# Twenty block products instead of twenty-two: the first layer of the last two experts as a rank-20 scheme

## The chip, the core and the metric

The kernel runs on one core of one Trainium2 chip. The metric is device time in microseconds of one execution. A core has TensorE (PE, with its weight loads PEld), VectorE (DVE), ScalarE (ACT), GpSimd (POOL) and SyncE (SP, here only a DMA queue). SBUF is the working memory, PSUM the eight banks into which matmuls accumulate.

## The reference, cut to what matters

A recurrent attention gives x (3072 tokens, 384 features); a mixture of four experts follows. The change touches only the second part, for experts 2 and 3:

```python
def _moe_ref(x, domain_probs, w1, w2) -> np.ndarray:
    N, D = x.shape                       # 3072, 384
    E = w1.shape[0]                      # 4 experts, 1024 hidden features each
    p = domain_probs / (domain_probs.sum(-1, keepdims=True) + 1e-09)
    out = np.zeros((N, D), dtype=np.float32)
    for e in range(E):
        h = np.maximum(x @ w1[e], 0.0)
        out += p[:, e:e + 1] * (h @ w2[e])
    return out.astype(np.float32)
```

All is float32. Each factor is split into a high part in a rounded format (F32R) and a low part, the rest; a product of two factors is three matmuls: high x high, low x high, high x low.

## The kernel before

**Two phases.** The first computes the attention and, beside it, experts 0 and 1 in blocks of 256 tokens (w1_step for the first layer, w2_step for the second; each step's second layer is issued one step late, and `mo.flush` issues the last). Sums of experts are kept in DRAM (acc_d). The second phase, from about 596 us on, does experts 2 and 3.

**Second phase.** Tokens come in blocks of 384 (TB2). A row R is a pair of such blocks for one expert; there are 4 rows per expert (NB2), 8 in all (NR2), R = 0 to 3 for expert 2 and R = 4 to 7 for expert 3. The 1024 hidden features are 8 tiles of 128. `unit(R, j)` takes two of these tiles and the pair of token blocks: a 2 x 3 matrix of 128 x 128 weight blocks times a 3 x 2 matrix of 128 x 384 blocks of x. Done directly that is 12 block products; a scheme with prepared sums of blocks (s1 to s4 of weights, t1 to t4 of x) needs 11. Each is `prod`, three matmuls of 384 columns. ScalarE and VectorE move partial results between four PSUM banks (a, b, c, d) and apply the ReLU: `hi_h` writes the high part of a hidden tile (ScalarE), `lo_h` the low part (VectorE).

**Second layer.** `l2(R, u, f)` multiplies one hidden tile of one token block by its second-layer weights: 9 matmuls into three output banks; after the eighth tile of a block VectorE adds the result, times the expert's probability, to the accumulator, which goes to acc2_d (expert 2, a GpSimd DMA) or out (expert 3, SP).

**Order.** All matmuls of the phase, and after the prologue all ScalarE and VectorE operations and the SP loads, are pinned in the order of the code. `fill(k)` puts an `l2` of an earlier unit between the products of a unit: four per unit from R = 1 on, two in row 0 and none in its first unit. The rest of the work, the preparation of weights (`prep_w`: loads, sums, splits) and of the next row's x (`prep_x`), stands in a list, `side`; `bg(n)` takes n steps from it at fixed points of a unit (`room`, `xat`, `late`). A split is a ScalarE copy to the high part and a VectorE subtraction for the low part. All weights of expert 2 and the x of row 0 are prepared in the prologue, beside the last block of the first phase. X's parts have two buffers each, hidden tiles twelve, PSUM has four banks for products and four for outputs.

Of the kernel before, what the change touches and what calls it, by code (L numbers as in the profile page):

```python
# [8 lines left out]
F32 = mybir.dt.float32  # L9
# [55 lines left out]
DMA_SCRATCH = 4096  # L65


def fast_path(ctx, tc, qkP, aP, vP, probsP, w, out, flag):
# [760 lines left out]
    with ExitStack() as c2:  # L829
        fin = c2.enter_context(tc.tile_pool(name="fin", bufs=2))  # L830
        ps_h2 = c2.enter_context(tc.tile_pool(name="ps_h2", bufs=2, space=PSUM))
        ps_o2 = c2.enter_context(tc.tile_pool(name="ps_o2", bufs=2, space=PSUM))
        acc2_d = [dram.tile([P, HD], F32, name=f"acc2_d{c}") for c in range(NT // P)]
        NP = FE // 2
        NR2 = (E - E1) * NB2
        pairs, shared = {}, {}
        count = {"h": 0, "o": 0, "w": 0}
        held = {"on": False}

        def cut(n):  # L840
            return slice(n * P, (n + 1) * P)

# [6 lines left out]
        def act(dst, src, fn=AF.Copy):  # L849
            pin(nc.scalar.activation(dst, src, fn))  # L850
# [7 lines left out]
        def split(hi, lo, src):  # L858
            return "split", (lambda: act(hi, src)), (lambda: tt(lo, src, hi, ALU.subtract))

        side = []

        def bg(n):
            while n > 0 and side:
                kind, first, second = side.pop(0)
                if kind == "split":
                    first()
                if kind != "sum" and side and side[0][0] == "split":
                    side[0][1]()
                    side[0] = ("rest",) + side[0][1:]  # L870
                second()
                n -= 1

        def stage2(i):
            tag = MID[count["w"] % len(MID)]
            count["w"] += 1
            return moe.tile([P, 2 * HD], F32, tag=tag, name=f"w2st{count['w']}", bufs=1 if tag == "x" else None)

        def prep_w(e, j):
            i = e * FE + 2 * j  # L880
            sts = []
            for u in range(2):
                st = stage2(i + u)
                pin(nc.sync.dma_start(st, w[i + u]))
                sts.append(st)
            st0, st1 = sts
            s = stage2(i)[:, :4 * P]
            if j % 2 == 0:
                shared[e] = [wpool.tile([P, 2 * HD], F32R, tag=f"w{nm}", name=f"s{nm}{i}") for nm in ("hi", "lo")]
            (h0, l0), (h1, l1) = ([wpool.tile([P, 2 * HD], F32R, tag=f"w{nm}", name=f"w{nm}{i + u}")  # L890
                                   for nm in ("hi", "lo")] for u in range(2))
            hs, ls = (x[:, (j % 2) * HD:(j % 2 + 1) * HD] for x in shared[e])

            def both(hi, lo, n):
                return hi[:, cut(n)], lo[:, cut(n)]

            pairs[e, j] = dict(a11=both(h0, l0, 0), a12=both(h0, l0, 1), a13=both(h0, l0, 2),
                               s4=both(h1, l1, 0), a22=both(h1, l1, 1), a23=both(h1, l1, 2),
                               s1=both(hs, ls, 0), s2=both(hs, ls, 1), s3=both(hs, ls, 2))
            wts[i], wts[i + 1] = (h0, l0), (h1, l1)  # L900

            def sums():
                tt(s[:, cut(0)], st1[:, cut(0)], st1[:, cut(1)], ALU.add)
                tt(s[:, cut(1)], s[:, cut(0)], st0[:, cut(0)], ALU.subtract)
                tt(s[:, cut(2)], st0[:, cut(0)], st1[:, cut(0)], ALU.subtract)
                tt(s[:, cut(3)], st0[:, cut(1)], s[:, cut(1)], ALU.subtract)

            return [("sum", None, sums), split(h0, l0, st0), split(h1[:, P:], l1[:, P:], st1[:, P:]),
                    split(hs, ls, s[:, :3 * P]), split(h1[:, cut(0)], l1[:, cut(0)], s[:, cut(3)])]

        def load_x2(R):
            xs = []
            for u in range(2):
                b = 2 * (R % NB2) + u
                x = fin.tile([P, NJ, TB2], F32, tag="x2", name=f"xb{R}_{u}", bufs=2)
                c = b * C2
                while c < (b + 1) * C2:
                    n = min(CG - c % CG, (b + 1) * C2 - c)
                    o = (c - b * C2) * P
                    pin(nc.sync.dma_start(x[:, :, o:o + n * P],  # L920
                                          y_d[c // CG].rearrange("(j p) t -> p j t", p=P)
                                          [:, :, c % CG * P:(c % CG + n) * P]))
                    c += n
                xs.append(x)
            return xs

        def prep_x(R, xs, X):
            (b11, b21, b31), (b12, b22, b32) = ([x[:, k, :] for k in range(NJ)] for x in xs)

            def put(nm, src):  # L930
                X[nm] = (fin.tile([P, TB2], F32R, tag="xoh", name=f"xh{R}_{nm}", bufs=9),
                         fin.tile([P, TB2], F32R, tag="xol", name=f"xl{R}_{nm}", bufs=9))
                return split(*X[nm], src)

            t2, t3 = (fin.tile([P, TB2], F32, tag=nm, name=f"{nm}_{R}", bufs=1) for nm in ("t2", "t3"))
            yield [("sum", None, lambda: tt(t3, b22, b12, ALU.subtract)),
                   ("sum", None, lambda: tt(b12, b12, b11, ALU.subtract)),
                   ("sum", None, lambda: tt(t2, b22, b12, ALU.subtract))]
            yield [put("b11", b11), put("t1", b12)]
            yield [put("t2", t2), put("b21", b21)]  # L940
            yield [("sum", None, lambda: tt(b21, b21, t2, ALU.subtract)), put("t3", t3), put("b22", b22)]
            yield [put("b31", b31), put("b32", b32), put("t4", b21)]

        def prod(ps, W, X, start=False, stop=False):
            (wh, wl), (xh, xl) = W, X
            for n, (a, b) in enumerate(((wh, xh), (wl, xh), (wh, xl))):
                pe(ps, a, b, start=start and n == 0, stop=stop and n == 2, skip_group_check=True)

        def claim(ps):
            pe(ps, pairs[E1, 0]["a11"][0], X["b11"][0], start=True, stop=True, skip_group_check=True)  # L950

        def bank(R, j, nm):
            count["h"] += 1
            return (ps_h, ps_h2)[count["h"] % 2].tile([P, TB2], F32, tag="ph", name=f"phb{R}_{j}{nm}")

        def temp(R, j, nm):
            return fin.tile([P, TB2], F32, tag="tmp", name=f"{nm}_{R}_{j}", bufs=5)

        hid = {}

        def hi_h(R, u, f, src):
            hh = fin.tile([P, TB2], F32R, tag="hh2", name=f"hhb{R}_{u}_{f}", bufs=12)
            act(hh, src, AF.Relu)
            hid[R, u, f] = hh, src
# [7 lines left out]
        def unit(R, j, X, fill, at):  # L972
# [5 lines left out]
            if R == 0 and j == 0:  # L978
                claim(b)
# [306 lines left out]
```

## Time and profile before

| | us |
|---|---|
| median of 3 runs | 992.63 (992.56 to 994.05) |
| the profiled execution | 992.13 |
| its span, first to last instruction | 990.4 |
| start of the second phase's matmuls | about 596.4 |
| the last matmul's end | about 984.1 |

The profiled execution is one run; its span leaves out 1.7 us around the program. Mean granted TensorE clock is 0.998. In rows of instruction groups the numbers are: count, busy time in us, mean ns of one, idle time of the engine before them and who ended it. In rows of single instructions they are: start in us, duration, engine, line, operation, tiles; idle time before it and its releaser stand in square brackets.

### The profile page before, as it was taken

What the parts mean: (1) busy time and instruction counts of PE and PEld (TensorE: products, weight loads), DVE (VectorE), ACT (ScalarE), POOL (GpSimd) and SP (SyncE); (2) the same over time, 40 slices, a digit from 0 to 9 for tenths busy, and PEclk for the clock granted to TensorE, in tenths of its full rate; (3) what the DMA queues carried; (4) which work ended last, traced back from release to release, by engine and by line L of the source; (5) the groups of instructions that cost most, each with busy time, mean ns of one, the idle gap of its engine ahead of it and who ended that gap; (6) DMA issues with size and microseconds to landing.
All of it is one profiled execution on the core that took longest, in us unless ns stands there. A gap on an engine that the chain in (4) does not pass through costs nothing.

```text
span 990.4 us, 17208 instructions
## 1 busy us (share of the span) xinstructions
PE 962.9 (97%) x6812; PEld 938.9 (95%) x6812; DVE 667.6 (67%) x1458; ACT 440.0 (44%) x856; POOL 52.7 (5%) x90
## 2 busy tenths in 40 slices
PE   5899998999999999999999999999999999999997
PEld 2799998999999999999999999999999999999997
DVE  7889989898888989878862374646454654444431
ACT  7755535355363643627232364434343534333320
POOL 6030000000000000000000000000000000000000
PEclk9999999999999999999999999999999999999999
DMA  9585276584665738366381453224131323131111
GB/s 312 170 172 138 71 188 144 142 190 123 176 157 136 179 129 208 107 167 175 74 184 17 130 154 116 72 67 133 49 118 59 107 70 96 48 96 49 49 48 51
DMA packets 102440, 120.63 MB, mean 122 GB/s; under 512 B 6928, under 2 KB 87872, under 8 KB 102352
## 3 DMA queue, kind: packets, MB, share of 16 engines
q1 hardware_dynamic: 95472, 98.83, 36.2%
q0 software_dynamic: 6880, 20.63, 8.5%
q8 instruction: 55, 0.90, 0.4%
q14 instruction: 33, 0.27, 0.1%
HBM read 78.81 MB, written 40.62 MB: 121 GB/s over the span
## 4 chain that ended last, share of the span: by engine, by line


## 5 line engine op out<-in xcount | busy, mean ns | idle before, releaser
L198 PE MATMUL po<-whi,hh 128*128 128x384 f32 x384 | 129.6, 338 | 1.1 <-ACT hh L188 1.1
L198 PE MATMUL po<-wlo,hh 128*128 128x384 f32 x384 | 128.9, 336 | 0.0
L847 PE MATMUL pob<-whi,hlb 128*128 128x384 f32 x384 | 128.3, 334 | 0.0
L847 PE MATMUL pob<-whi,hhb 128*128 128x384 f32 x384 | 128.3, 334 | 0.0
L847 PE MATMUL pob<-wlo,hhb 128*128 128x384 f32 x384 | 128.3, 334 | 0.0
L198 PE MATMUL po<-whi,hl 128*128 128x384 f32 x384 | 124.3, 338 | 1.0 <-DVE hl L189 1.0
L188 ACT ACTIVATE hh<-ph 128x512 fp32r<-128x512 f32 x96 | 57.1, 594 | 145.4 <-PE ph L178 142.8
L178 PE MATMUL ph<-xha,whi 128*128 128x256 f32 x576 | 103.9, 286 | 1.2 <-ACT xha L165 1.2
L178 PE MATMUL ph<-xha,wlo 128*128 128x256 f32 x576 | 101.3, 283 | 0.0
L178 PE MATMUL ph<-xla,whi 128*128 128x256 f32 x576 | 100.9, 284 | 0.4 <-DVE xla L167 0.4
L189 DVE SCALAR_TENSOR_TENSOR hl<-ph,hh 128x512 fp32r<-128x512 f32 x96 | 66.0, 688 | 44.2 <-ACT hh L188 43.6
L178 PEld LDWEIGHTS ph<-xha,whi 128*128 128x128 f32 x576 | 85.9, 190 | 2.5 <-ACT xha L165 1.5
L178 PEld LDWEIGHTS ph<-xla,whi 128*128 128x128 f32 x576 | 82.5, 191 | 0.6 <-DVE xla L167 0.6
L178 PEld LDWEIGHTS ph<-xha,wlo 128*128 128x128 f32 x576 | 82.8, 190 | 0.2 <-issue 0.2
L198 PEld LDWEIGHTS po<-whi,hh 128*128 128x128 f32 x384 | 72.4, 189 | 1.5 <-ACT hh L188 1.3
L198 PEld LDWEIGHTS po<-whi,hl 128*128 128x128 f32 x384 | 70.9, 188 | 2.3 <-DVE hl L189 2.2
L198 PEld LDWEIGHTS po<-wlo,hh 128*128 128x128 f32 x384 | 72.5, 189 | 0.0
L847 PEld LDWEIGHTS pob<-whi,hhb 128*128 128x128 f32 x384 | 72.1, 188 | 0.0
L847 PEld LDWEIGHTS pob<-wlo,hhb 128*128 128x128 f32 x384 | 72.1, 188 | 0.0
L847 PEld LDWEIGHTS pob<-whi,hlb 128*128 128x128 f32 x384 | 72.1, 188 | 0.0
L532 PE MATMUL sc<-Qst,Kst 112*128 112x128 f32 x384 | 49.9, 280 | 0.8 <-DMA Qst<-q_d 0.3
L559 ACT ACTIVATE y<-yp 48x512 f32<-48x512 f32 (+1 forms) x42 | 24.9, 592 | 55.5 <-PE yp L553 55.2
(384 smaller groups left out, 1979.9 us busy)
## 6 DMA issues: line engine op xcount, KB each, us to landing
qk<-qkP SPq DMA_DIRECT2D x24, 384.0 KB, 6.9
acc_d<-acc POOLq DMA_DIRECT2D x24, 384.0 KB, 4.8
acc<-acc_d SPq DMA_DIRECT2D x48, 192.0 KB, 2.5
A<-aP SPq DMA_DIRECT2D x22, 384.0 KB, 8.1
w2st<-w SPq DMA_DIRECT2D x16, 384.0 KB, 3.8
xb<-y_d SPq DMA_DIRECT2D x16, 384.0 KB, 4.4
q_d<-Q SPq DMA_DIRECT2D x12, 387.0 KB, 4.1
Qst<-q_d SPq DMA_DIRECT2D x12, 387.0 KB, 5.9
```

What stands on the lines that cost most here:

```text
L178: ins = nc.tensor.matmul(ph[:, u, :], wt[:, j * P:(j + 1) * P], xt[:, j, :], start=(n == 0), stop=(n == 3 * NJ - 1))
L188: wts["hh"] = nc.scalar.activation(hh, ph, AF.Relu)
L189: nc.vector.scalar_tensor_tensor(hl, ph, 0.0, hh, op0=ALU.max, op1=ALU.subtract)
L198: nc.tensor.matmul(po[t], ht[:, u, t * P:(t + 1) * P], wt[:, HD:], start=(i % FE == 0 and n == 0), stop=(i % FE == FE - 1 and n == 2))
L532: ins = nc.tensor.matmul(s_ps[:, h, :], Kc[:, hf * 4 + h, :], Qc[:, hf * 4 + h, :], start=True, stop=True)
L559: state["y", g, c] = nc.scalar.activation(y[us, :, cs], y_ps[us], AF.Copy)
L847: return tc.keep_in_program_order(nc.tensor.matmul(*args, **kw))
```

## The change

Only the second phase changes.

- A unit now takes four feature tiles and the pair of token blocks: a 4 x 3 matrix of weight blocks times a 3 x 2 matrix of blocks of x, as 20 products (before: two units of 11). XOF says which of 16 prepared parts of x a product uses; UNIT is the order of one unit, written out: `M` product (number, bank, whether it starts the bank), `C` ScalarE copy, `D` VectorE sum, `H` and `L` the high and low parts of a hidden tile, `F` one `l2`, `B` steps from the side list. A unit has 20 `M`, 8 `C`, 10 `D`, 8 `H`, 8 `L`, 8 `F`.
- The first unit, (0, 0), has no `l2`; its first `F` is the flush.
- Of the sums of x, 12 per row, all are on GpSimd and not pinned; 16 splits per row. The parts X have one buffer each: a part is split anew (`need`, `freed`) only after its last product in the row's second unit.
- `prep_w` prepares the first-layer weights of one half expert: 4 loads, 14 block sums, 6 splits; its second-layer weights come by a GpSimd DMA, a negating ScalarE copy and an accumulating GpSimd DMA. Only the first half of expert 2 is prepared in the prologue; the second half in unit (0, 0), expert 3's halves in units (1, 0) and (4, 0).
- Raw weights, their sums, raw x and the sums of x share one tile, Z. In those three units the x of the next row is loaded behind the weights' steps in the side list; what is left in the list is drained at the end of each unit with h = 0.
- Five PSUM banks for products, three for outputs, each fixed; hidden tiles in a ring of eleven.

```diff
+XOF = (0, 1, 2, 3, 4, 5, 6, 7, 0, 8, 9, 6, 10, 11, 12, 13, 14, 15, 5, 9)
+UNIT = (
+    ("M", 19, 0, True), ("C", 1, 0),
+    ("M", 10, 2, True),
+    ("F",), ("B", 3),
+    ("M", 6, 0, False), ("C", "A", 0),
+    ("M", 11, 1, False), ("C", 3, 1), ("B", 2),
+    ("F",), ("D", 4, "A", "-", 2),
+    ("M", 1, 0, False), ("C", "B", 0),
+    ("M", 7, 3, False), ("H", 2, 0, 3),
+    ("M", 16, 1, False), ("C", "D", 1), ("L", 2, 0, 3),
+    ("F",), ("B", 3),
+    ("M", 12, 4, False), ("H", 0, 0, 4),
+    ("M", 3, 2, False), ("D", "B", "B", "-", 2),
+    ("M", 17, 0, False), ("C", "C", 0, -1.0), ("L", 0, 0, 4),
+    ("M", 8, 1, False), ("C", "E", 1),
+    ("F",), ("B", 4),
+    ("M", 13, 2, False), ("D", 3, 2, "-", "D"), ("D", "F", 2, "-", "E"),
+    ("M", 0, 0, True), ("C", "A", 0),
+    ("M", 2, 1, True), ("D", 4, 1, "+", "C"),
+    ("F",), ("D", 2, "A", "-", 1), ("B", 2),
+    ("M", 9, 3, False), ("H", 1, 0, 3),
+    ("M", 5, 0, False), ("L", 1, 0, 3), ("D", "F", "F", "-", 0),
+    ("F",), ("D", 1, 0, "+", "B"), ("H", 1, 1, "F"), ("B", 2),
+    ("M", 15, 4, False), ("H", 3, 0, 4),
+    ("M", 18, 2, False), ("L", 1, 1, "F"), ("L", 3, 0, 4), ("D", 3, 2, "+", "E"),
+    ("F",), ("D", "C", "C", "-", 2), ("B", 3),
+    ("M", 14, 1, False), ("H", 0, 1, 1), ("H", 3, 1, "C"),
+    ("F",), ("L", 0, 1, 1), ("L", 3, 1, "C"),
+    ("M", 4, 3, False), ("H", 2, 1, 3), ("B", 2), ("L", 2, 1, 3),
+)
...
+        Z = fin.tile([P, 11 * TB2], F32, name="Z")
+        X = [tuple(fin.tile([P, TB2], F32R, name=f"x{nm}{n}") for nm in ("h", "l")) for n in range(16)]
...
+        def pool(dst, x, y, op):
+            nc.gpsimd.tensor_tensor(dst, x, y, op=op)
...
         def bg(n):
-            while n > 0 and side:
-                kind, first, second = side.pop(0)
+            while side:
+                kind, need, first, second = side[0]
+                if need is not None and need not in freed:
+                    return
+                if kind != "pool" and n <= 0:
+                    return
+                if kind == "gap" and first > 0:
+                    side[0][2] -= 1
+                    return
+                side.pop(0)
+                if kind == "gap":
+                    continue
+                if kind in ("pool", "sum", "act"):
+                    first()
+                    n -= kind != "pool"
+                    continue
                 if kind == "split":
                     first()
-                if kind != "sum" and side and side[0][0] == "split":
-                    side[0][1]()
-                    side[0] = ("rest",) + side[0][1:]
+                if side and side[0][0] == "split" and (side[0][1] is None or side[0][1] in freed):
+                    side[0][2]()
+                    side[0][0] = "rest"
                 second()
                 n -= 1
...
+        def prep_w(e, h, base, raw, sums):
...
+            out = [step(*[(u,) for u in range(4)], on=load), ["gap", None, 2, None],
+                   step((n(0, 4), raw[:, :, 1], raw[:, :, 0], sub)),
+                   step((n(10, 12), raw[:, 2, :2], raw[:, 3, :2], add), (s[:, 8], a(1, 3), a(4, 3), add)),
+                   step((s[:, 9], a(2, 3), a(3, 3), add), (n(4, 6), n(0, 2), raw[:, :2, 2], add)),
+                   step((n(6, 8), n(0, 2), n(8, 10), add), (s[:, 5], s[:, 5], a(4, 3), sub)),
+                   step((s[:, 12], a(1, 2), a(2, 1), add), (s[:, 8], s[:, 12], s[:, 8], add),
+                        (s[:, 9], s[:, 12], s[:, 9], sub)),
+                   step((s[:, 10], s[:, 6], s[:, 10], sub), (s[:, 11], s[:, 7], s[:, 11], add)),
+                   step((s[:, 13], a(3, 1), a(4, 2), add), (s[:, 14], a(3, 1), a(1, 2), sub))]
+            for src, q, lim in ((n(0, 6), 0, slice(0, 6)), (n(6, 12), 1, slice(0, 6)), (n(12, 15), 2, slice(0, 3)),
+                                (raw[:, 2, 0::2], 2, slice(3, 5)), (a(2, 1), 2, 5)):
+                out.append(split(blocks(hi[q], lim), blocks(lo[q], lim), src))
+            out.append(split(blocks(ext, slice(0, 2)), blocks(ext, slice(2, 4)), raw[:, 3, 1:3], mark=("w", e, h)))
...
+                def minus(d_hi=d_hi, d_lo=d_lo, k=i + u):
+                    nc.gpsimd.dma_start(d_hi, w[k][:, HD:])
+                    act(d_lo, d_hi.bitcast(F32), scale=-1.0)
+                    nc.gpsimd.dma_start(d_lo, w[k][:, HD:], accum_op=ALU.add)
...
+        def prep_x(R):
+            b11, b21, b31, b12, b22, b32, v7, v6, v9, ta, tb = (Z[:, wide_cut(n)] for n in range(11))
...
+            return [step((R,), on=load_x2),
+                    g((v7, b11, b21, add), (ta, b12, b31, add), (v6, b22, b32, sub), (v9, b31, v6, add),
+                      (tb, b11, b31, add)),
+                    put(9, v7), put(6, b31), put(1, ta, True),
+                    g((ta, v7, v6, sub), (b31, b31, b32, sub), (b32, b12, b32, add)),
+                    put(7, b21), put(14, v9, True),
+                    g((b21, b21, v9, sub), (v7, v7, b12, sub)),
+                    put(10, tb, True),
+                    g((tb, v7, b22, sub)),
+                    put(3, ta), put(15, b12),
+                    g((b11, b12, b11, sub)),
+                    put(11, v6), put(0, b31), put(8, b21), put(12, b32), put(2, v7), put(5, tb), put(13, b11),
+                    put(4, b22)]
...
+        late_w = {(0, 0): (E1, 1, 5), (1, 0): (E1 + 1, 0, 10), (NB2, 0): (E1 + 1, 1, 0)}
+        freed.update(range(16))
+        side += prep_x(0)
+        drain()
+        side += prep_w(E1, 0, 0, SN[:, :4 * HD], ACC[:, :15 * P])
+        drain()
         held["on"] = True
...
+            for h in range(2):
+                if h == 1 or R > 0:
+                    acc_load(R if h == 1 else R - 1, 1 - h)
+                if (R, h) in late_w:
+                    e, q, base = late_w[R, h]
+                    side += prep_w(e, q, base, Z[:, :4 * HD], Z[:, 4 * HD:4 * HD + 15 * P])
+                if h == 0 and R + 1 < NR2:
+                    todo_x = prep_x(R + 1)
+                    side += todo_x[:2]
+                elif R + 1 < NR2:
+                    freed.clear()
+                    side += todo_x[2:]
+
+                def fill(k, first=(R == 0 and h == 0)):
+                    if not first:
+                        l2()
+                    elif k == 0:
+                        mo.flush()
+
+                unit(R, h, fill)
+                if h == 0:
+                    drain()
+        acc_load(NR2 - 1, 1)
+        for _ in range(FE):
+            l2()
```

## What I predict and why

> **What bounds the kernel now.** I read the busy shares first, then the stretches, then TensorE's waits, then single instructions. The page of the kernel before:
>
> ```profile
> span 990.4 us, 17208 instructions
> PE 962.9 (97%) x6812; PEld 938.9 (95%) x6812; DVE 667.6 (67%) x1458; ACT 440.0 (44%) x856; POOL 52.7 (5%) x90
> PE   5899998999999999999999999999999999999997
> DVE  7889989898888989878862374646454654444431
> ```
>
> TensorE is busy in nearly every slice; VectorE falls to about half of that in the second phase (from slice 24). The stretches split the second phase into its first row of blocks (R = 0) and a little of the next, and the rest; the last is the exit. Columns: stretch, length, then busy time and count of TensorE's matmuls, its weight loads, VectorE, ScalarE and GpSimd, the granted clock, DMA share and GB/s.
>
> ```profile
> 596.40:648.80 52.40, 51.59 (x290) 49.85 (x290) 27.11 (x54) 24.66 (x53) 2.50 (x4) 1.00 0.28 85
> 648.80:984.10 335.30, 335.30 (x1935) 334.99 (x1933) 159.76 (x312) 119.46 (x255) 11.23 (x21) 1.00 0.23 73
> 984.10:990.40 6.30, 0.01 (x1) 0.00 (x0) 0.67 (x2) 0.00 (x0) 0.00 (x0) 0.90 0.30 101
> ```
>
> From 648.8 on TensorE never pauses: 335.30 / 1933 weight loads = 0.1735 us per matmul, whatever it multiplies. So a matmul taken out is worth 0.1735 us as long as the other engines keep up. The waits of TensorE from 560 on are two, both tiny, and one of the phase's few gaps shows how a chain through VectorE stalls it in the first row, where little second-layer work is there to fill:
>
> ```profile
> PE phb_3b L847 <- DVE phb_3c L853: 0.3, 1, 0.3
> 605.38 0.19 PEld L847 LDWEIGHTS phb_1d<-xh_t,shi 128*128 128x128 f32 x1 [0.45 <-DVE mq L853]
> ```
>
> **The change, part by part. Matmuls.** Before, the phase issues 32 pairs x 33 = 1056 first-layer matmuls, 2 that claim a bank, 1152 second-layer ones and the 12 of the first phase's last step (flush): 2222, which are the weight loads of the two rows, 290 + 1933, but for one at the seam. Dense they take 2222 x 0.1735 = 385.5 us; the stretch takes 387.7, so 2.2 are gaps. After: 16 units x 60 + 3 + 1152 + 12 = 2127, dense 369.0 us. Against 387.7 that is **18.7 us to gain**, if TensorE never waits. The question is only what waits appear.
>
> Prices of the other engines:
>
> ```profile
> L853 DVE TENSOR_TENSOR xl_b<-xb,xh_b 128x384 fp32r<-128x384 f32 x40 | 21.4, 552 | 2.0 <-ACT xh_b L850 1.1 <-DMA xb<-y_d 0.9
> L853 DVE TENSOR_TENSOR wlo<-w2st,whi 128x768 fp32r<-128x768 f32 x8 | 7.6, 956 | 5.7 <-ACT whi L850 5.6
> L853 DVE TENSOR_TENSOR w2st<-w2st,w2st 128x128 f32<-128x128 f32 x24 | 6.0, 287 | 0.9 <-DMA w2st<-w 0.7
> 571.71 0.55 DVE L853 TENSOR_TENSOR xl_t<-t,xh_t 128x384 fp32r<-128x384 f32 x1
> 572.18 0.55 DVE L853 TENSOR_TENSOR xl_b<-xb,xh_b 128x384 fp32r<-128x384 f32 x1
> 570.45 0.52 ACT L850 ACTIVATE xh_b<-xb 128x384 fp32r<-128x384 f32 x1
> 570.86 0.51 ACT L850 ACTIVATE xh_t<-t 128x384 fp32r<-128x384 f32 x1
> L856 DVE SCALAR_TENSOR_TENSOR acc<-pob,pr,acc 128x384 f32<-128x384 f32 x48 | 26.7, 612 | 25.0 <-PE pob L847 24.0 <-DMA xb<-y_d 0.9
> ```
>
> Back to back a 384-wide operation starts 0.47 us after the last on VectorE, 0.41 on ScalarE; by width VectorE takes 0.08 less than the mean duration: 0.21 (128), 0.34 (256), 0.47, 0.60 (512), 0.87 (768).
>
> **An ordinary unit** (four features, two token blocks): 60 + 72 matmuls x 0.1735 = 22.9 us. VectorE does 10 sums, 8 `L`, up to 16 splits and 3 accumulations: 34 x 0.47 + 3 x 0.6 = 17.8; ScalarE 32 x 0.41 = 13.1. Both fit. I followed UNIT in order with these prices: with second-layer work (1.56 us) at each `F`, no product waits; the tightest is product M9, due at 15.1 us, whose bank 3 comes from a VectorE sum (`3 = 2 - D`) that ends at 13.6. So the units run dense, but for the four below.
>
> **Unit (0,0)** has no second-layer work except the flush; dense it has 75 matmuls, 13.0 us. VectorE there does 18 operations of the unit (8.5), 14 block sums of the next half's weights (20 blocks wide in all: 3.7) and their 6 splits (3.1): 15.3 us, in program order. Its first can start at about 5.0, after the flush and the copy of bank 0 behind it. The product M4 needs the second `3 = 2 + E` sum, behind which 2.4 us of VectorE work are left: 5.0 + 15.3 - 2.4 = 17.9, plus 1.5 in which VectorE waits for copies: 19.4, and M4 ends at 20.0. **Loss 7.0** (5.6 without those waits, 7.5 with a little more).
>
> **Rows of x behind the weights.** In the three units that prepare weights, (0,0), (1,0), (4,0), the loads of the next x stand in the side list behind the last weight split, since both use Z. By the fixed numbers in UNIT the last two splits come in the final `B`. In (1,0) and (4,0) VectorE has 8.5 + 3.7 + 3.1, three leftover splits of x (1.4) and the accumulations (1.8): 18.5 of 22.9 us, but bunched late. Followed in order, it reaches the three splits before M14 at 21.5 us, the accumulations at 23.2, two `L` at 24.9 and is through the last splits at 26.1, 3.2 after TensorE's end. The next unit's first split (v7, a GpSimd sum) stands on ScalarE ahead of the copies of bank 0 and bank 1, which products M1 and M7 wait for. How long x takes:
>
> ```profile
> 562.06 1.97 SPq L920 DMA_DIRECT2D xb<-y_d  x4
> 566.10 0.53 ACT L850 ACTIVATE xh_b<-xb 128x384 fp32r<-128x384 f32 x1 [1.09 <-DMA xb<-y_d]
> DMA to landing us min/median/max: 3.1/4.3/8.6
> L258 POOL MEMSET P<- 112x384 f32 x1 | 0.4, 412 | 0.0
> L263 POOL TENSOR_SCALAR_AFFINE_SELECT band<-band 48x288 f32<-48x288 f32 x2 | 1.4, 694 | 0.1
> ```
>
> The first block is there 4.0 us after the first issue. No row shows a two-input sum on GpSimd. From below, the memset of 384 columns, 0.41; from above, the select scaled to 384 columns, 694 x 384 / 288 = 0.93. It reads as well as writes, so I take 0.9. The Trainium skill (GPSIMD Engine Reference, section 3.1) gives 4497 ns for 2048 fp32 columns; by that an estimate for 384 would be near 0.9 too.
>
> Unit (1,1): splits done at 3.2, x at 7.2, v7 at 8.1, its copy started at 8.15, bank 0's copy done at 9.05, M1 at 9.1. Without the wait M1 would come at 5.2, so 3.9 are lost, in (4,1) likewise; in (0,1), where VectorE isn't behind, the same sum gives 1.2. **Loss 9.0** (6.3 at the shortest landing, 5.2 with a GpSimd sum of 0.5 as well, 11 where POOL's queue holds v7 for 1 us twice: the weights' DMAs below).
>
> A pause of that size also costs clock. The start of this trace has one:
>
> ```profile
> 27.13 3.11 PE L390 MATMUL qp<-Q,wide 128*64 128x128 f32 x26 [2.65 <-DVE Q L430]
> 25.00:26.00 1.00, 0.00 (x0) 0.00 (x0) 0.38 (x1) 0.94 (x3) 0.00 (x0) 1.00 1.17 393
> 26.00:27.00 1.00, 0.00 (x0) 0.00 (x0) 0.96 (x4) 0.36 (x2) 0.00 (x0) 0.77 1.21 418
> 27.00:28.00 1.00, 0.87 (x6) 0.87 (x8) 0.95 (x5) 0.87 (x2) 0.00 (x0) 0.50 1.16 396
> 28.00:29.00 1.00, 1.00 (x14) 1.00 (x12) 1.00 (x4) 0.23 (x1) 0.00 (x0) 0.50 0.57 191
> 29.00:30.00 1.00, 1.00 (x14) 1.00 (x12) 1.00 (x4) 0.00 (x0) 0.00 (x0) 0.53 0.05 18
> ```
>
> After 2.65 us without a matmul the granted clock is 0.50 until about 29.5. Some 2.8 us at half clock lose 1.4, and I count it behind the two long pauses: **loss 2.8** (0 to 4.2).
>
> **GpSimd against VectorE.** 12 sums per row move off VectorE: 12 x 0.9 = 10.8 us in 45.8, so GpSimd has room. VectorE's splits read two SBUF operands beside them. No row of before has both at once. From below 0; from above each of 7 sums in a second unit holds up one split by a whole 0.9, which brings the sum before M9 from 13.6 to 16.0 and costs 1.0 in each of 7 units: 7. I take 0, since 1.5 us of cover must go first.
>
> The Trainium skill speaks against that choice (SBUF — State Buffer, section "SBUF: two separate sides"): a VectorE instruction with two SBUF inputs and a GpSimd one that reads SBUF exclude each other for their whole length. No run shown has the two together; by it the sum would lie towards the rival of contention below.
>
> **The second layer's weights** come by GpSimd DMA with a ScalarE negation between:
>
> ```profile
> L131 POOL DMA_DIRECT2D wlo<-w x8 | 7.2, 970 | 16.7 <-ACT wlo L130 16.7
> L126 POOL DMA_DIRECT2D whi<-w x8 | 4.3, 558 | 1.3 <-DMA maskp<-mask_d 1.2
> 557.98 1.86 SPq L884 DMA_DIRECT2D w2st<-w  x2
> ```
>
> That is 4 x 0.56 + 4 x 0.97 = 6.1 us of POOL's queue in each of the three units; the accumulating four follow the copies and so stand just ahead of v7. The first four aren't pinned; unpinned loads went out early before (557.98, 38 us ahead of their use), so I cost the waits at nothing and four 0.41 copies a unit on ScalarE, under cover. The acc loads on SP stand behind x and are due 20 us later. First and last moments stay: the phase starts with the flush, and 6.3 us after the last matmul are the same stores. The prologue does less on VectorE (16 + 6 splits and 14 small sums for 25 splits and 20 sums), and its GpSimd sums have 30 us.
>
> **The sum.** -18.7 + 7.0 + 9.0 + 2.8 + 0 = +0.1. The profiled execution took 992.13 (span 990.4 and 1.7 around it), 0.5 under the median of the runs; so 992.2 for it and, between the two bases, **992.5**: no change, because the waits eat the 96 matmuls.
>
> **Rivals.**
> *No loss of clock* (faster): the pauses are real, but TensorE's work around them keeps the clock up. 992.2 - 2.8 = 989.4. For it: one pause in one place is all the trace has to judge by; against: the two pauses here are longer than that one.
> *Early x* (faster): loads land at 3.1, GpSimd sums take 0.5, so losses are 7.0 + 5.2, and with the pauses under 2.7 no clock is lost: 992.1 - 6.5 = 985.6. Against: Z orders the loads behind the splits, whatever their speed.
> *The change doesn't do what it says* (slower): the count drops, but matmuls from the new tiles take longer. The one price of 0.1735 over all kinds of products speaks against; each 1% of it is 3.7 us, and 5% would undo the gain.
> *Contention* (slower). GpSimd sums and splits exclude each other; above 1.5 us of delay per second unit M9 waits: 7 x 1.0 so 992.2 + 7 = 999. It decides as soon as two splits are each held by a whole GpSimd sum.
> *Weight copies wait* (slower). If the first DMAs of the second layer's weights go out only where they are written in the code, ScalarE waits several us in each of three units, over 1002.
>
> **How the numbers follow.** As summed, within 0.2% (2 us, about what a measurement can tell from no change): 0.29. No loss of clock 0.20 and early x 0.17: faster 0.37. Contention 0.18, the longer ends of the waits 0.10, weight copies 0.04, slower products 0.02: slower 0.34. The lowest ends of the losses together are 5.6 + 5.2 = 10.8 and give 984.2; the highest, 7.5 + 11 + 4.2 + 7 = 29.7, give 1003.1. They will hardly all meet, so the range is 984.5 to 1001.5; the likeliest case alone has 990.5 to 994.5.
>
> **What would show it.** About 2127 matmuls in the phase at 0.1735. TensorE waits on VectorE in the first 20 us of the phase (7 us); waits on ScalarE's copy of the bank early in the second, fourth and tenth unit, with x's DMA behind them and clock under 1.0 after two of them; dense elsewhere. Waits spread over every unit would mean contention; a first unit of under 16 us would break the largest step, and x landing well before the last split would break the next.

## The result, and the profile after

The changed kernel takes 1018.77 us (median of 4 runs, 1014.26 to 1020.73) where the kernel before took 993.34 (4 runs, 992.56 to 994.56): a ratio of 1.0248 [1.0212, 1.0285]. Forecast was no change, 992.5, and the range ended at 1001.5. The profiled execution took 1014.26. (One execution of run 10 below took 1342.21 us at a mean granted clock of 0.66; it is left out of that run's ratio.) The page of the profiled execution:

```profile
span 1012.6 us, 17537 instructions
PE 958.2 (95%) x6717; PEld 930.9 (92%) x6717; DVE 748.3 (74%) x1594; ACT 479.3 (47%) x952; POOL 181.4 (18%) x218
PE   5899999999999999999999897988999979999997
PEclk9999999999999999999999899998999999999999
```

TensorE does 95 matmuls fewer and ends 22.2 us later by the span. Behind the first two slices, in which it isn't full before either, the slices in which it isn't full are few, and in two of them its granted clock is lower as well. So the loss isn't spread; it sits in some stretches. Here they are, first the last block of the first phase (from the first load of the second phase's x to the phase's first matmul), then the phase as a whole, then its parts. Columns as in the prediction.

```profile
562.80:604.46 41.66, 36.71 (x240) 35.91 (x241) 28.61 (x45) 18.41 (x38) 21.15 (x22) 0.92 0.51 124
604.46:1006.10 401.64, 378.88 (x2128) 374.18 (x2127) 262.25 (x507) 183.22 (x400) 122.64 (x133) 0.97 0.29 84
604.46:625.00 20.54, 15.04 (x79) 13.54 (x79) 14.48 (x37) 11.77 (x26) 3.92 (x6) 0.99 0.28 59
625.00:650.00 25.00, 22.83 (x121) 22.01 (x121) 17.49 (x29) 12.02 (x28) 16.32 (x15) 0.94 0.47 126
677.00:700.00 23.00, 16.09 (x75) 15.20 (x74) 11.42 (x18) 9.05 (x21) 17.27 (x18) 0.78 0.60 158
700.00:820.00 120.00, 120.00 (x693) 120.00 (x693) 84.35 (x169) 58.05 (x126) 35.85 (x44) 1.00 0.25 78
820.00:850.00 30.00, 21.82 (x110) 20.54 (x109) 18.88 (x30) 12.69 (x29) 18.73 (x19) 0.89 0.41 106
```

The same last block in the kernel before, with the same 241 weight loads:

```profile
562.06:596.41 34.35, 34.14 (x240) 33.82 (x241) 23.58 (x52) 18.27 (x36) 1.43 (x2) 1.00 0.59 171
```

A stretch's loss is its length less 0.1735 us for each weight load. The phase has 2127 of them, 369.0 us, in 401.64: 32.6 lost. By parts: 6.8 in unit (0,0), 4.0 in (0,1), 10.2 around (1,1), 11.1 around (4,1), and nothing from 700 to 820. Another 7.3 (41.66 - 34.35) went in the last block of the first phase, before any changed matmul. Against the 387.7 of before, the sum is 7.3 + (401.6 - 387.7) + 0.9 at the two ends = 22.1.

TensorE's waits from 555 to the phase's start, and from 590 on (total, times, longest):

```profile
PE po L229 <- DVE hl L220: 4.9, 2, 4.3
```

```profile
PE pb L883 <- ACT SN L886: 13.5, 2, 6.9
PE pb L883 <- DVE pb L889: 7.4, 5, 2.2
PE pb L883 <- DVE SN L889: 1.5, 2, 0.8
```

**The last block of the first phase.** TensorE waits for `hl`, a VectorE operation of the first phase. The timeline ahead of that wait, GpSimd's and VectorE's rows by turns:

```profile
569.85 3.61 POOL L895 TENSOR_TENSOR Z<-Z 128x384 f32<-128x384 f32 x3 [0.47 <-DMA Z<-y_d]
571.22 2.66 DVE L889 TENSOR_TENSOR xl<-Z,xh 128x384 fp32r<-128x384 f32 x2
574.03 1.27 POOL L895 TENSOR_TENSOR Z<-Z 128x384 f32<-128x384 f32 x1
573.80 1.86 DVE L889 TENSOR_TENSOR ACC<-SN 128x128 f32<-128x128 f32 x2
578.60 1.01 PE L229 MATMUL po<-whi,hl 128*128 128x384 f32 x2 [4.32 <-DVE hl L220]
```

Two splits, which took 0.55 us each in the kernel before, take 2.66 beside GpSimd's sums of row 0, and two small sums of weights, of a kind that takes 0.28 elsewhere in this block, take 1.86. `hl` stands behind them on VectorE and starts only at 577.87. TensorE's waits are 4.9 of the 7.3 us lost; most of the rest is clock, 0.50 from the end of the longer wait to about 583.6, some 2.5 us by an estimate from windows of 1 us.

**Unit (0,1).** Its 4.0 us aren't a wait for x: no product waits for ScalarE there. Part of it, some 1.4 us, is half clock left over from the waits of (0,0), until about 627.8. The rest are two waits for VectorE, 0.75 and 1.42, and the second is that of product M9, which the prediction named as the tightest:

```profile
632.13 11.86 POOL L895 TENSOR_TENSOR Z<-Z 128x384 f32<-128x384 f32 x10 [0.30 <-DMA Z<-y_d]
640.49 2.65 DVE L889 TENSOR_TENSOR xl<-Z,xh 128x384 fp32r<-128x384 f32 x2
643.66 0.44 PE L883 MATMUL pb<-xh,shi 128*128 128x384 f32 x1 [1.42 <-DVE pb L889]
```

The two splits, of a kind of which two take 1.01 us at 644.92, stand just ahead of the VectorE sum that fills M9's bank. The 1.6 us more that they take beside GpSimd's sums are more than M9's wait.

**The long pauses.** The chain behind the one in (1,1), by engine: SP loads x and then ACC, GpSimd's queue has the accumulating DMAs of the second layer's weights, GpSimd sums, ScalarE copies, TensorE waits.

```profile
676.16 1.84 POOL L994 DMA_DIRECT2D slo<-w  x2
677.51 2.08 SPq L1012 DMA_DIRECT2D Z<-y_d  x4
679.69 7.64 SPq L1085 DMA_DIRECT2D ACC<-acc_d  x6
685.09 1.94 POOL L895 TENSOR_TENSOR Z<-Z 128x384 f32<-128x384 f32 x2 [4.15 <-issue]
686.11 0.52 ACT L886 ACTIVATE xh<-Z 128x384 fp32r<-128x384 f32 x1 [8.63 <-POOL Z L895]
687.07 0.69 PE L883 MATMUL pb<-xh,shi 128*128 128x384 f32 x1 [6.63 <-ACT SN L886]
```

The windows around it:

```profile
680.00:690.00 10.00, 3.37 (x12) 3.05 (x11) 1.90 (x4) 2.70 (x6) 4.43 (x6) 0.62 1.07 305
690.00:700.00 10.00, 10.00 (x50) 9.68 (x50) 8.26 (x11) 5.87 (x13) 9.84 (x9) 0.87 0.05 18
```

These two places are those foretold; the size isn't. The first block of x comes 7.6 us after its issue (677.51 to 685.09), with the DMA engines full at 305 GB/s, and after the pause the clock stays below full until some 2.6 us into the second of the two stretches (0.13 x 10 us / 0.5).

**GpSimd's prices.** The sums and the splits of x over the whole run:

```profile
L895 POOL TENSOR_TENSOR Z<-Z 128x384 f32<-128x384 f32 x96 | 105.4, 1122 | 123.0 <-DMA Z<-y_d 65.6
L889 DVE TENSOR_TENSOR xl<-Z,xh 128x384 fp32r<-128x384 f32 x104 | 70.2, 705 | 37.7 <-ACT xh L886 32.1
```

A sum is 1.12 us in the mean where 0.9 was taken; a split is 0.705 in the mean where 0.552 was measured before.

### The profile page after: what moved, and what is told of

Read it like the earlier page. It is cut to its first block, busy times and chain, and to the rows that moved or that the text cites. A ratio compares the mean times of both kernels' runs of the same rounds, so it can differ in the third digit from the quotient of the medians.

```text
span 1012.6 us, 17537 instructions
## 1 busy us (share of the span) xinstructions
PE 958.2 (95%) x6717; PEld 930.9 (92%) x6717; DVE 748.3 (74%) x1594; ACT 479.3 (47%) x952; POOL 181.4 (18%) x218
## 4 chain that ended last, share of the span: by engine, by line
## 5 line engine op out<-in xcount | busy, mean ns | idle before, releaser
L883 PE MATMUL pob<-shi,hid 128*128 128x384 f32 x528 | 149.7, 338 | 0.0
L895 POOL TENSOR_TENSOR Z<-Z 128x384 f32<-128x384 f32 x96 | 105.4, 1122 | 123.0 <-DMA Z<-y_d 65.6
L883 PE MATMUL pb<-xh,shi 128*128 128x384 f32 x291 | 99.7, 344 | 22.8 <-ACT SN L886 13.5
L883 PEld LDWEIGHTS pob<-shi,hid 128*128 128x128 f32 x528 | 98.5, 192 | 0.0
L889 DVE TENSOR_TENSOR xl<-Z,xh 128x384 fp32r<-128x384 f32 x104 | 70.2, 705 | 37.7 <-ACT xh L886 32.1
L883 PE MATMUL pb<-xh,slo 128*128 128x384 f32 x288 | 97.9, 340 | 0.0
L883 PE MATMUL pb<-xl,shi 128*128 128x384 f32 x288 | 97.8, 340 | 0.0
L883 PE MATMUL pob<-slo,hid 128*128 128x384 f32 x264 | 89.3, 338 | 0.0
L883 PEld LDWEIGHTS pb<-xh,shi 128*128 128x128 f32 x291 | 55.5, 191 | 27.0 <-ACT SN L886 14.4
L886 ACT ACTIVATE xh<-Z 128x384 fp32r<-128x384 f32 x128 | 60.6, 516 | 35.5 <-POOL Z L895 33.7
```

Of the source, the lines that this page charges most:

```text
L883: return tc.keep_in_program_order(nc.tensor.matmul(*args, **kw))
L886: return pin(nc.scalar.activation(dst, src, fn, scale=scale))
L889: pin(nc.vector.tensor_tensor(dst, x, y, op=op))
L895: nc.gpsimd.tensor_tensor(dst, x, y, op=op)
```

## The experiments

The theory (A in all expectations) was that four separate things lose the time: GpSimd's sums hold VectorE's splits in the last block of the first phase; VectorE bounds unit (0,0); x lands late in three units, because its load waits for the weights in Z and then shares the DMA engines; and the clock falls after the long pauses. The rivals differ by run. Ten kernels ran; lines of code below are those of the changed kernel.

**1. Row 0's sums of x on VectorE.**

```diff
             def g(*ops):
-                return step(*ops, on=pool)
+                return step(*ops) if R == 0 else step(*ops, on=pool)
```

> The 12 sums of x of row 0 (prologue) on VectorE; all else as changed. Theory A (GpSimd sums and VectorE's two-operand splits shut each other out, and ScalarE and VectorE stand in order behind them, so the last block of the first phase stalls): the second phase's first matmul comes at 596.5 to 598 instead of 604.5, splits of the prologue take 0.55 us, time about 7 us lower (1011 to 1012). Rival B (the order in which the prologue was put into the streams, not the port): still 603 or later, time 1017 to 1020.

Measured: 1013.18 (2 runs), ratio 1.0191 [1.0142, 1.0239]. The stretch of the last block, and its one wait left:

```profile
565.57:601.27 35.70, 34.08 (x240) 33.76 (x241) 25.23 (x57) 18.22 (x38) 7.23 (x10) 1.00 0.58 144
```

```profile
578.67 0.61 PE L229 MATMUL po<-whi,hl 128*128 128x384 f32 x2 [1.62 <-DVE hl L220]
```

35.70 instead of 41.66: 6.0 of the 7.3 lost us are back, waits and half clock alike, although VectorE has more to do. So it was not VectorE's load but GpSimd beside it. (In this execution the stretch began 2.8 us later than in the other, which hides part of that in the span.) The phase starts at 601.3, later than theory A had it and earlier than the rival, and the time lies 1.2 us above theory A's.

**2. A gap of three background steps before the splits of x in the three late units.**

```diff
                     freed.clear()
+                    if R in (0, 1, NB2):
+                        side.append(["gap", None, 3, None])
                     side += todo_x[2:]
```

> In the three rows whose x is loaded behind weights, the first splits of x stand three side steps later. Theory A (ScalarE, in order, stands in front of x and holds the copy of bank 0): the two pauses of 6.6 and 6.9 us go, and with them the low clock; 15 to 20 us lower, 998 to 1003. Rival B (TensorE needs that x soon anyway, so the wait only moves to a later product): pauses of 4 us or more appear later in the same units, 1010 or more.

Measured: 1007.90 (2 runs), 1.0138 [1.0090, 1.0186]. The pauses of 6.6 and 6.9 on ScalarE are gone, since the bank copies now stand ahead of the first split. VectorE is late next:

```profile
693.56 0.44 PE L883 MATMUL pb<-xh,shi 128*128 128x384 f32 x1 [3.09 <-DVE pb L889]
```

The losses there fall to about 6 each: the splits, moved back, are now late themselves and hold up VectorE. So some four tenths of the loss was the order on ScalarE. The time lies between the two expectations.

**3. No accumulating DMA for expert 3's second-layer weights.** Left out is the low part of those weights.

```diff
                     act(d_lo, d_hi.bitcast(F32), scale=-1.0)
-                    nc.gpsimd.dma_start(d_lo, w[k][:, HD:], accum_op=ALU.add)
+                    if e == E1:
+                        nc.gpsimd.dma_start(d_lo, w[k][:, HD:], accum_op=ALU.add)
```

> The accumulating GpSimd DMA of expert 3's second-layer weights is left out (their low part is then wrong), nothing else. Theory A (x lands 7.6 us after issue because those transfers run at the same time): x is there 4.0 to 5.0 us after its first issue in units (1,1) and (4,1), both pauses shrink to about 3.5, time 8 us lower (1009 to 1011). Rival B (stores and loads of the accumulators, or the load itself): landing 7 or more, 1016 to 1019.

Measured: 1009.47 (2 runs), 1.0153 [1.0096, 1.0211]. In unit (1,1):

```profile
681.43 2.02 SPq L1013 DMA_DIRECT2D Z<-y_d  x4
685.68 1.94 POOL L895 TENSOR_TENSOR Z<-Z 128x384 f32<-128x384 f32 x2 [4.57 <-DMA Z<-y_d]
```

x lands 4.25 us after its issue instead of 7.6, and the two pauses are 3.33 and 3.37, not far from the 3.9 of the prediction, which had x land in 4.0; the time is theory A's. The accumulating DMAs cost x some 3.4 us each time. Whether by their bytes or because they accumulate, or come from GpSimd's queue, this run doesn't separate.

**4. All sums of x on VectorE.**

```diff
-                return step(*ops, on=pool)
+                return step(*ops)
```

> All sums of x on VectorE, GpSimd has none. Theory A (port): the splits of x are back at 0.55 us on the mean (0.70 as changed), the delay of the second phase's start is gone as in the first experiment, the rows without weights stay dense although VectorE has 5.6 us more per row; about 1008 to 1012. Rival B (VectorE was the reason to use GpSimd: it falls behind and TensorE waits in every row): 1018 or more, waits on VectorE in all rows.

Measured: 1035.74 (2 runs), 1.0418 [1.0338, 1.0497], the slowest of all. Its groups and its waits:

```profile
L889 DVE TENSOR_TENSOR xl<-Z,xh 128x384 fp32r<-128x384 f32 x104 | 53.9, 550 | 10.6 <-ACT xh L886 9.7
L889 DVE TENSOR_TENSOR Z<-Z 128x384 f32<-128x384 f32 (+3 forms) x138 | 62.2, 489 | 48.5 <-DMA Z<-y_d 47.4
```

```profile
PE pb L883 <- DVE pb L889: 25.1, 10, 5.1
```

The splits are back at 0.55, so the longer ones were GpSimd's doing. But VectorE's operations are pinned in order, and a sum that waits for x's DMA (47.4 us in all) now stands in front of TensorE's operands: in the first unit of each of rows 2, 3, 5 and 6, dense before, TensorE waits once for 4.4 to 5.1 us. The time is the rival's, though the waits aren't in all rows. For the rows as a whole the sums are better off on GpSimd; row 0, in the prologue, is the exception.

**5. The second half of expert 2's weights prepared in the prologue**, the negations left in (0,0).

```diff
-        late_w = {(0, 0): (E1, 1, 5), (1, 0): (E1 + 1, 0, 10), (NB2, 0): (E1 + 1, 1, 0)}
+        late_w = {(1, 0): (E1 + 1, 0, 10), (NB2, 0): (E1 + 1, 1, 0)}
...
+        first_w = prep_w(E1, 1, 5, Z[:, :4 * HD], Z[:, 4 * HD:4 * HD + 15 * P])
+        side += first_w[:-4]
+        drain()
         held["on"] = True
...
                     side += todo_x[:2]
+                    if R == 0:
+                        side += first_w[-4:]
```

> The second half of expert 2's weights is summed and split in the prologue, behind row 0's x, instead of in unit (0,0); the four negations for its second-layer weights stay in (0,0). Theory A (unit (0,0) is bound by VectorE, and the pause in (0,1) is x landing behind the weights in Z): VectorE has some 10 us free from 593 to 604, the preparation is 7.4 us long, so the 6.8 us lost in the first 20.5 us of the phase fall to under 1.5 and the 4.0 lost in (0,1) to under 1.5; 1008 to 1012 in all. Rival B (the work only moves into the last block of the first phase): the waits there on hl grow from 4.9 by about as much, and the time stays at 1015 to 1020.

Measured: 1008.27 (4 runs), 1.0139 [1.0103, 1.0174]. In the two units of row 0 three short waits remain (0.90, 0.55 and 0.82), together 2.3 us where 6.8 and 4.0 were lost, and the time is theory A's. The rival has a small share: the last block of the first phase, from x's first load at 563.54 to the first matmul at 606.66, grew from 41.7 to 43.1.

**6. x's load ahead of the negations** in (1,0) and (4,0), which go to the head of the next unit.

```diff
-                    side += prep_w(e, q, base, Z[:, :4 * HD], Z[:, 4 * HD:4 * HD + 15 * P])
+                    now = prep_w(e, q, base, Z[:, :4 * HD], Z[:, 4 * HD:4 * HD + 15 * P])
+                    keep = now[-4:] if R else []
+                    side += now[:-4] if R else now
...
+                    if R in (1, NB2):
+                        side += keep
                     side += todo_x[2:]
```

> In units (1,0) and (4,0) the four negations with their eight GpSimd DMAs go to the head of (1,1) and (4,1), so that x's load is issued four background steps earlier and ahead of the accumulating DMAs. Theory A (the two long pauses are x's landing, its late issue and its 7.6 us under the accumulating DMAs): x's load issued about 4 us earlier and landed within 4.3 us, so the ScalarE waits of 6.6 and 6.9 go, the losses of 10.2 and 11.1 us fall to 1 to 4 each; 1003 to 1007 in all. Rival B (GpSimd's sums in front of the first splits are what is late): VectorE waits of about 3 us take their place, as with a gap before the splits; losses 6 each, 1009 to 1012.

Measured: 1017.59 (4 runs), 1.0231 [1.0185, 1.0276]: no gain, and outside what either side expected.

```profile
680.15 2.03 SPq L1012 DMA_DIRECT2D Z<-y_d  x4
692.15 11.54 POOL L895 TENSOR_TENSOR Z<-Z 128x384 f32<-128x384 f32 x10 [5.72 <-DMA Z<-y_d]
696.30 0.69 PE L883 MATMUL pb<-xh,shi 128*128 128x384 f32 x1 [4.98 <-DVE SN L889]
```

The first two sums start at 684.46, but the third waits for x until 692.15, 12.0 us after the issue: the negations' DMAs now fall on the rest of x instead of on its start. The load itself didn't move: it goes out 0.1 us after the start of a product at 680.04, and in the changed kernel within 0.1 us of the same product (677.53), since the last weight split comes in the unit's final step anyway. So only the transfers around x moved, and the wait with them.

**7. Edits 1, 5 and 6 together.**

> Three edits together: row 0's sums of x on VectorE, the second half of expert 2's weights in the prologue, and the negations of units (1,0) and (4,0) behind x's load. Theory A (the losses are separate and add up: 7.3 in the last block of the first phase, 6.8 in (0,0), 4.0 in (0,1), 10.2 and 11.1 around the two pauses): some 2 to 3 us are left of each of two or three places, 981 to 988 and so faster than before. Rival B (the prologue's VectorE is now the bound, with 20 + 14 sums and 25 splits beside the last block): the first phase's last block grows by 4 to 8 us, 990 to 996.

Measured: 1000.07 (6 runs), 1.0066 [1.0043, 1.0089], above both expectations. Most of what was left is around x's landing: waits of 1.51 and 4.75 us in (1,1), of 1.77 and 2.45 in (4,1). The DMA view of this kernel from 660 to 690 (queue's issues, KB each, median us to landing):

```profile
DMA packets 3233, 3.74 MB, mean 125 GB/s; under 512 B 272, under 2 KB 3088, under 8 KB 3232
ACC<-acc_d SPq DMA_DIRECT2D x6, 192.0 KB, 9.7
Z<-y_d SPq DMA_DIRECT2D x2, 384.0 KB, 6.9
slo<-w POOLq DMA_DIRECT2D x4, 192.0 KB, 8.1
```

x is 1.18 MB (the two issues shown and two of 192 KB), the ACC loads are as much again, the accumulating DMAs 0.79 and three stores of the accumulator 0.59. In this kernel the third sum starts at 677.63, 12.0 us after x's issue at 665.67, with all these bytes beside it.

**8. The negations out of the way**: as 7, but those of (1,0) go into (2,0), those of (4,0) behind x's sixth step in (4,1).

```diff
                     side += todo_x[:2]
...
+                    if R == 2:
+                        side += keep
...
-                    if R in (1, NB2):
-                        side += keep
                     side += todo_x[2:]
+                    if R == NB2:
+                        side[6:6] = keep
```

> As the three together, but the negations of unit (1,0) with their eight DMAs go into (2,0), and those of (4,0) into the middle of (4,1), behind x's sixth step; x's load stays four steps earlier. Theory A (the landing of x is a matter of bytes: behind 665.67 in the kernel with the three edits 3.74 MB were moved at some 0.26 MB per us, and the last quarter of x came after about 12 us): x's 1.18 MB with the ACC loads of 0.6 to 1.2 MB land within 4.3 to 7 us, GpSimd's ten sums start by about 672 in (1,1), the waits of 4.75 and 2.5 us there go, the losses around the two units fall from 8.8 and 5.6 to 2 or 3 each; 988 to 993 in all, 7 to 12 us under the kernel with the three edits. Rival B (GpSimd's twelve sums of 1.0 to 1.4 us in front of the splits are the limit whenever x lands at the start of a unit): the waits on VectorE stay at 2 us or more each; 996 to 1000.

Measured: 1002.61 (5 runs), 1.0098 [1.0081, 1.0115]: a miss, above both expectations. x lands in 4.36 us, as the theory has it, but its load goes out at the unit's end as before; and the moved negations are late for the second layer:

```profile
815.33 0.69 PE L883 MATMUL pb<-xh,shi 128*128 128x384 f32 x1 [3.69 <-ACT SN L886]
832.66 0.69 PE L883 MATMUL pob<-slo,hid 128*128 128x384 f32 x1 [5.89 <-DMA slo<-w]
```

**9. x's load between the weight splits**: as 8, but the raw weights lie in the part of Z that x's load doesn't write, the load goes out ahead of the last three weight splits, and the negations of (4,0) are at the head of (4,1).

```diff
-                    now = prep_w(e, q, base, Z[:, :4 * HD], Z[:, 4 * HD:4 * HD + 15 * P])
+                    now = prep_w(e, q, base, Z[:, 6 * TB2:10 * TB2], Z[:, :15 * P])
                     keep = now[-4:]
-                    side += now[:-4]
+                    side += now[:-7]
...
-                    side += todo_x[:2]
+                    side += todo_x[:1]
+                    if (R, h) in late_w:
+                        side += now[-7:-4]
+                    side += todo_x[1:2]
...
-                    side += todo_x[2:]
                     if R == NB2:
-                        side[6:6] = keep
+                        side += keep
+                    side += todo_x[2:]
```

> As the kernel before it in this list, with two differences. The weights of (1,0) and (4,0) lie in the part of Z that x's load doesn't write, so that the load goes out ahead of their last three splits; and the negations of (4,0) are at the head of (4,1) again, since the second layer waited 5.9 us for them. Theory A (what is left is x's landing of 4.3 us behind a load that still goes out at the end of the unit, and that one wait of 5.9): issued 3 to 4 us earlier, x has landed when the unit ends, the two ScalarE waits of 3.7 fall under 1 and with them the half clock behind them; 986 to 992 in all. Rival B (GpSimd's sums are late in any case): VectorE waits of 2 to 3 us remain in both units, 993 to 998.

Measured: 990.18 (11 runs), 0.9973 [0.9962, 0.9983] against 993.07. The phase as a whole, and the largest wait left in it:

```profile
599.36:980.35 380.99, 371.83 (x2128) 368.20 (x2127) 257.50 (x487) 180.57 (x394) 119.23 (x129) 1.00 0.29 86
```

```profile
822.48 0.44 PE L883 MATMUL pb<-xh,shi 128*128 128x384 f32 x1 [2.70 <-DVE pb L889]
```

The loss of 32.6 us has become 12.0, and the mean clock of the phase 1.00; the time is theory A's. The step from run 8 is two moves at once, x's load and the negations of (4,0); the wait of 5.9 us belongs to the second, and how the rest divides wasn't tried.

**10. As 9, with the seven later sums of x in rows 2 and 5 on VectorE.**

```diff
-            def g(*ops):
-                return step(*ops) if R == 0 else step(*ops, on=pool)
+            def g(*ops, late=True):
+                return step(*ops, on=tt if R == 0 or late and R in (2, NB2 + 1) else pool)
...
-                      (tb, b11, b31, add)),
+                      (tb, b11, b31, add), late=False),
```

> As the kernel with x's load between the splits, but in rows 2 and 5 (prepared in (1,1) and (4,1)) the seven later sums of x are VectorE's, the first five stay on GpSimd. Theory A (what is left there, 0.76 and 1.42 us in (1,1), 1.86 and 2.70 in (4,1), are VectorE splits held while GpSimd's back-to-back sums have the port: VectorE is busy 6.00 of 6.00 us with 6 instructions): seven sums at 0.55 are 3.9 us more for VectorE, the ten splits beside them lose their holds, and the four waits fall to under 2 us together; 985 to 988. Rival B (VectorE is simply full in these units, whoever sums): the waits stay or grow; 990 to 994.

Measured: 988.44 (7 runs), 0.9949 [0.9928, 0.9970] against 993.58, a median between the two expectations. By the interval it is faster than the kernel before, by half a per cent, and it has the lowest ratio of all, though its interval overlaps that of run 9.

```profile
600.78:980.15 379.37, 371.61 (x2128) 368.17 (x2127) 256.94 (x501) 180.56 (x394) 102.62 (x115) 1.00 0.29 86
```

```profile
817.49 0.45 PE L883 MATMUL pb<-xh,shi 128*128 128x384 f32 x1 [2.53 <-DVE SN L889]
```

The waits in the two late units fell only from 6.7 to 5.3, not under 2. Holds by GpSimd are part of what is left and VectorE's own work another; how much of each wasn't settled.

## Why the prediction was wrong, point by point

- **The gain: right.** 2127 weight loads, and 0.1735 us each in dense stretches (693 in 120.00).
- **Unit (0,0), 7.0: right**, in size (6.8) and in mechanism: all its waits are on VectorE (four, 5.5 us together), and run 5 takes most of them away by moving the preparation out. It foresaw one long wait, not four, and no clock lost behind them.
- **Ordinary units dense: right.** From 700 to 820 TensorE never pauses, although the splits there share the time with GpSimd's sums. Taking contention as 0 holds for these units.
- **"The prologue ... its GpSimd sums have 30 us": wrong, 7.3 us.** This is the step that failed outright. GpSimd did have the time; what it cost was VectorE's, in a stretch where the first phase's second layer needs `hl` from VectorE. The contention was weighed for the phase's units alone and left out where the sums lie beside the first phase. The Trainium skill (SBUF — State Buffer, section "SBUF: two separate sides") was the side to take there: an instruction with two SBUF inputs on VectorE and one on GpSimd that reads SBUF exclude each other, and the one that starts first keeps the port for its whole length. The rows agree, 2.66 us for two splits of 0.55, and run 1 shows the price.
- **Rows of x behind the weights: the right places, the wrong size.** The term was mis-sized in its landing of 4.0 us: 7.6 in (1,1) and 7.9 in (4,1). The losses around those two units are 21.3 where 7.8 was put, or 10.6 with the clock's 2.8. The 4.0 came from a row in which x was alone. The eight DMAs of the second layer's weights were costed as time in GpSimd's queue, not as transfers that x shares the DMA engines with; without the accumulating half x lands in 4.25 and the pauses are 3.3 and 3.4 (run 3). In (0,1), 4.0 us were lost where 1.2 was put, and by another mechanism: not ScalarE waiting for x, but splits held beside GpSimd's sums, and half clock from (0,0).
- **Half clock: right that it comes, too small.** (In the row that the prediction reads, 29.00:30.00 at 0.53, half clock ends near 29.9, not 29.5; its 2.8 us fit the former.) The clock was 0.50 for some 5.5 us of matmuls behind the pause in (1,1) (from 687.07 to about 692.6), so 2.7 lost at one pause, which is nearly what was counted for both. The one in (4,1) lost some 2.2, and two more places had it that weren't counted at all: behind `hl` (2.5) and behind the waits of (0,0) (1.7), estimates from windows of 1 us. A longer pause let more of the work behind it fall into the slow stretch; that the length of the pause alone sets it isn't shown (see below).
- **The rivals.** Contention came, mostly at another place than the rival had it: in the first phase. The waits of M9 that it foretold came in two units of seven, 1.42 us in (0,1) and 1.23 in (4,1). The late weight copies didn't come: those of (1,0) had their first DMAs out at 652.83, 22 us before the copies at 675.35, and no such copy waited for a DMA. The range left out the upper ends, which "will hardly all meet"; but a late landing lengthens the pause, and the clock's loss came with the longer pause, so those two did meet. Even all upper ends together gave only 1003.1, since the first phase's block isn't among them.

Between forecast (+0.1) and result (+22.2 by the span) lie 7.3 in the first phase's last block, 2.8 in (0,1), 10.7 in the two late units (21.3 - 10.6), 0.9 at the two ends and 0.5 in small waits elsewhere, less 0.2 in (0,0): 22.0.

What is slow is the preparation around the scheme, not its products. With the same 2127 matmuls, row 0's sums off GpSimd, the second weights prepared ahead of the phase and x's load ahead of the last weight splits, the kernel is 0.3% faster than the one before (run 9), with seven more sums off GpSimd 0.5% (run 10). The rest of the 18.7 us is still lost: in run 10, 10.4 in the phase (379.37 - 369.0), and the phase starts 4.4 us later than before (600.78 against 596.41).

## What to carry to other kernels

Price a moved operation at every place where it runs, and by what shares a port or a DMA engine with it there, not by whether its own engine has time. A landing time read from a quiet row can be far too short, here 4.0 us for 7.6: look at what other queues have under way when the load goes out. And when work is put onto a shared buffer, place the load that the next stage waits for by the last read of the region it overwrites, not by the last read of the whole tile.

## What the runs showed of the hardware

**A split can wait through several sums.** In run 3, unit (0,1), VectorE's and GpSimd's rows:

```profile
634.40 4.33 DVE L889 TENSOR_TENSOR xl<-Z,xh 128x384 fp32r<-128x384 f32 x1 [0.41 <-PE pb L883]
634.13 4.18 POOL L895 TENSOR_TENSOR Z<-Z 128x384 f32<-128x384 f32 x4
```

The split began 0.27 us after the first of four back-to-back sums and ended after the fourth: 4.33 us for 0.55 of work. In other places of the same kernel a split gets in after one sum (1.35).

**The clock falls after some pauses only.** In run 7 a wait of 1.77 us that ended at 821.93 was followed by half clock; in run 9 a wait of 2.70 us that ended at 822.48 was not. Windows of run 7, then of run 9, behind these waits:

```profile
822.00:823.00 1.00, 1.00 (x4) 1.00 (x5) 1.00 (x2) 0.14 (x1) 0.88 (x1) 0.57 1.14 257
823.00:824.00 1.00, 1.00 (x5) 1.00 (x4) 0.82 (x2) 0.84 (x2) 1.00 (x2) 0.50 1.15 255
```

```profile
823.00:824.00 1.00, 1.00 (x8) 1.00 (x7) 1.00 (x3) 0.49 (x1) 0.00 (x0) 1.00 0.00 0
```

Nor was a wait of 2.45 us in run 7 itself, ended at 833.70, with the clock at 1.00 behind it. So length alone doesn't decide. What else does wasn't tried.
